# LSH attention into a soft mixture of experts: work on key tiles placed one by one, a 72-column transpose operand, and a new issue order

## The chip, the cores and the metric

The kernel runs on one core of one Trainium2 chip. The metric is the device time of one execution in microseconds (us); less is better. The engines are PE (TensorE; PEld is its weight load), DVE (VectorE), ACT (ScalarE), POOL (GpSimd) and SP (SyncE, which issues the DMAs here).

## What is computed

For each of B·H = 32 heads (S = 768 tokens, D = 64) queries and keys are hashed to 6 sign bits by a projection. A query attends only to keys with the same six bits:

```python
mask = q_bucket[:, :, :, None] == k_bucket[:, :, None, :]
scores = scale * np.matmul(q, k.transpose(0, 1, 3, 2))
scores = np.where(mask, scores, -1000000000.0)
attn = softmax(scores)            # with 1e-9 in the denominator
x = attn @ v                      # then (3072, 512)
logits = x @ phi                  # 8 experts x 4 slots
slot_input = softmax(logits, axis=0).T @ x
slot_out[e] = relu(slot_input[e] @ w1[e]) @ w2[e]
out = softmax(logits, axis=1) @ slot_out
```

## The kernel before

**Tiling.** The 768 keys of a head are six tiles of 128. Scores are held with keys on partitions and queries along the row, so that the exponentials go straight into the product with v. Heads are worked on in pairs (an even one and the odd one after it), since a transfer of queries and keys brings both. The 512-column PSUM buffers hold pieces of 512, 256 + 256 and 512 columns of two key tiles.

**Steps of a head.** `load` brings a pair's queries and keys. `bits` (line 328, four 32-column products in a 32-column shape of the array) and line 321 make the hash signs. `split_hi` (ACT, line 290) and `split_lo` (DVE, line 294) split the values into a rounded high part and a low rest in the tile w (w4); the `spread_*` DMAs (issued at line 298) lay these and the bits out in one of three operand tiles XY. `smax` (line 370) computes a first round of masked scores, whose maxima DVE reduces (lines 373 and 376) into mx. `shift` (lines 382, 383, 385, DVE) makes from mx a 128-row tile mz of 12 columns, six with the negative maximum and six with a large number where nothing matched. `shift_rows` turns mz by a transpose (line 404), ACT copies the turned rows (line 407), and a DMA puts them as one row into XY, so that the second product, `scores` (line 419), has the shift in it. ACT takes the exponential (line 423) into three tiles pt, each for two key tiles. `acc` keeps the running sum of the exponentials over key tiles on GpSimd (line 429 for the first two, line 435 for the others); `av` multiplies them with v (line 446, two 64-column halves of the array) and ACT copies the result (line 450).

**Steps of a pair.** `pair_sum` (line 458) sums over partitions, `pair_turn` (493), `pair_rec` (465), `pair_log` (473), `pair_add` (485, 487) and `pair_x` (508 on PE, 510 on DVE) divide by the sum and make x and its logits. After each eight heads the `batch_*` steps fold a batch into running slot inputs. Behind the last head come the experts (lines 829 to 953). Their weights are loaded by SP while the heads run, as buffers come free.

**The order.** Nothing is scheduled by a compiler. Every step is entered by `at` into a list with a number, its place in units of one key tile (six a head), the list is sorted, and each engine gets its instructions in that order and works through them in it. The table WHEN holds the numbers relative to a head's first slot (two lists where even and odd heads differ), FIRST replaces some of them for the first and the last heads. `acc` and `av` are entered three times a head, once for each two key tiles.

Of the kernel before, what the change touches and what calls it, by code (L numbers as in the profile page):

```python
# [44 lines left out]
WHEN = {'load': -23.228,
 'bits': -14.718,
 'split_hi': -14.15,
 'split_lo': [-13.173, -12.657],
 'spread': [[-13.185, -11.633, -9.493, -7.304], [-10.44, -10.41, -11.057, -10.018]],
 'load_v': [-3.955, -4.754],  # L50
 'smax': [[-7.721, -7.546, -7.104, -6.759, -6.183, -5.672, -5.543, -5.94, -4.42, -4.667, -3.989, -3.458],
          [-7.807, -7.787, -7.71, -7.157, -7.093, -4.763, -4.509, -5.317, -2.787, -3.873, -3.838, -5.786]],
 'scores': [[-0.379, -0.64, 0.722, 1.221, 1.676, 1.813, 4.783, 5.371, 5.128, 2.397, 4.882, 5.891],
            [0.479, 0.475, 0.687, 1.928, 1.817, 1.633, 2.087, 3.051, 4.451, 4.142, 4.29, 3.884]],
 'shift': [-2.803, -2.153],
 'shift_rows': [-2.18, -2.143],
 'acc': [[4.764, 7.001, 8.685], [3.578, 3.949, 8.203]],
 'av': [[3.488, 6.789, 7.032], [3.202, 4.62, 6.466]],
 'pair_sum': 15.98,
 'pair_turn': 17.963,  # L60
 'pair_rec': [18.062, 18.408, 18.445],
 'pair_log': 18.701,
 'pair_x': [22.593, 24.311],
 'pair_add': 19.165,
 'batch_both': 21.266,
 'batch_max': 21.916,
 'batch_exp': 22.194,
 'batch_turn': 23.394,
 'batch_scale': 23.246,
 'batch_slots': 24.562,  # L70
 'batch_weigh': 24.425,
 'batch_share': 28.126,
 'load_weights': 4.18}

FIRST = {('load', 4): 4.476,
 ('bits', 2): 1.288,
 ('split_hi', 2): 0.833,
 ('split_lo', 2, 0): 1.029,
 ('split_lo', 2, 1): 2.366,
 ('spread_y', 2): 1.587,  # L80
 ('spread_bits', 2): 1.668,
 ('spread_l', 2): 2.667,
 ('spread_x', 2): 3.34,
 ('smax', 1, 0, 0): -1.746,
 ('smax', 1, 0, 1): -1.169,
 ('smax', 1, 1, 0): 0.452,
 ('smax', 1, 1, 1): 0.57,
 ('smax', 1, 2, 0): 1.478,
 ('smax', 1, 2, 1): 1.593,
 ('smax', 1, 3, 0): 2.035,  # L90
 ('smax', 1, 3, 1): 2.061,
 ('smax', 1, 4, 0): 2.241,
 ('smax', 1, 4, 1): 2.696,
 ('smax', 1, 5, 0): 2.774,
 ('smax', 1, 5, 1): 3.433,
 ('one_sum', 30): 189.395,
 ('one_log', 30): 188.431,
 ('one_fold', 3): 189.992,
 ('one_turn', 30): 189.777,
 ('one_rec', 30): 190.438,  # L100
 ('one_add', 30): 190.708,
 ('one_x', 30): 191.23,
 ('one_put', 30): 192.78,
 ('acc', 31, 2): 192.109,
 ('av', 31, 2, 0): 191.864,
 ('av', 31, 2, 1): 192.733,
 ('first_y', 1): -20.551,
 ('first_y', 2): -3.524,
 ('spread_y', 1): -14.012,
 ('spread_l', 0): -12.047,  # L110
 ('spread_bits', 1): -7.869,
 ('bits_rest',): -7.878,
 ('bits_copy',): -13.916}


def constants():
# [31 lines left out]
def lsh_attention_soft_moe(  # L148
# [228 lines left out]

    def shift(h):
        s = st[h]
        mz = mp.tile([P, 2 * NT], F32, name="mz", bufs=2)  # L380
# [1 line left out]
        nc.vector.tensor_reduce(out=m, in_=s["mx"], axis=AX.X, op=ALU.max)
        nc.vector.tensor_scalar(out=mz[:, NT:2 * NT], in0=m, scalar1=NOMATCH, scalar2=BIG,  # L383
                                op0=ALU.is_lt, op1=ALU.mult)
        nc.vector.scalar_tensor_tensor(out=mz[:, 0:NT], in0=m, scalar=-1.0, in1=mz[:, NT:2 * NT],
                                       op0=ALU.mult, op1=ALU.subtract)
        s["mz"] = mz

    def shift_rows(h):
        s = st[h]  # L390
# [13 lines left out]
        nc.tensor.transpose(pt[0:2 * NT, 0:P], s["mz"], ident)  # L404

        mr = mp.tile([2 * NT, P], F32R, name="mr", bufs=1)
        nc.scalar.copy(mr, pt[0:2 * NT, 0:P])  # L407
        move(s["XY"][ROW:ROW + 1, 0].rearrange("o y (t p) -> o (y t) p", p=P), mr)
# [14 lines left out]
            nc.scalar.activation(s["P", i // 2][:, 512 * u:512 * u + 512], pt, AF.Exp, scale=D ** -0.5)  # L423

    def acc(h, j):
        s = st[h]
        pr = s["P", j]
        if j == 0:
            nc.gpsimd.tensor_tensor(out=s["acc"], in0=pr[:, 0:S], in1=pr[:, S:2 * S], op=ALU.add)  # L429
        else:  # L430
            for a in range(2):
                n = 2 * j + a
                eng = nc.vector if h == BH - 1 and n > 2 else nc.gpsimd
                if h < BH - 1 or n < NT - 1:
                    eng.tensor_tensor(out=s["acc"], in0=s["acc"], in1=pr[:, a * S:(a + 1) * S], op=ALU.add)  # L435

    def av(h, j, half=None):
        s = st[h]
        if j == 0:
            s["av"] = p_av.tile([P, 512], F32, name="av")  # L440
        pr = s["P", j]
        for i in (2 * j, 2 * j + 1):
            o = (i % 2) * S
            for c in range(2):
                if half in (None, i % 2):
                    nc.tensor.matmul(s["av"][64 * c:64 * c + 64, 0:HC], s["v"][:, i, :],  # L446
                                     pr[:, o + c * HC:o + (c + 1) * HC], start=(i == 0), stop=(i == NT - 1))
# [277 lines left out]
    for h in range(BH):  # L725
        s0, x = NT * h, h % 2
        if x == 0:
            if h > 0:
# [8 lines left out]
        for n in range(2 * NT):
# [1 line left out]
            at(s0 + WHEN["scores"][x][n], scores, h, n // 2, n % 2)  # L739
        at(s0 + WHEN["shift"][x], shift, h)  # L740
        at(s0 + WHEN["shift_rows"][x], shift_rows, h)
        for j in range(NT // 2):
            lone = h == BH - 1 and j == NT // 2 - 1
            at(s0 + (5.725 if lone else WHEN["acc"][x][j]), acc, h, j)
            if lone:
                for n in range(2):
                    at(s0 + 5.85 + n, av, h, j, n)
            else:
                at(s0 + (WHEN["av"][x][j] if h < BH - 1 else (3.513, 5.087)[j]), av, h, j)
# [257 lines left out]
```

## Time and profile before

| | us |
|---|---|
| time, median of 3 runs | 516.64 (516.59 to 516.72) |
| span of the profiled execution | 515.0, 1.64 less than that median |
| PE busy | 494.8 (96%) |
| DVE busy | 381.7 (74%) |
| GpSimd (POOL) busy | 327.6 (64%) |
| ACT busy | 241.2 (47%) |

The profiled execution is one run of its own, of which the profiler gives the span: from the first instruction to the end of the last, without what lies around it in a run's time. Busy times of an engine are those of its instructions; they overlap between engines, and matmuls are pipelined, so that on PE the distance from one start to the next says more than a duration. [...]

### The profile page before, as it was taken

Reading aid. Unit: us, or ns where it says so; the run is one execution under the profiler, and the core shown is the slowest. Engines: PE = TensorE matmul, PEld = TensorE weight load, DVE = VectorE, ACT = ScalarE, POOL = GpSimd, SP = SyncE. Lnnn points to the kernel's source line nnn. Section 1 sums busy time; section 2 is a strip of 40 time slices with the busy share of each in tenths; the row PEclk is TensorE's granted clock in tenths of the full one; section 3 lists DMA queues with packets and bytes.
Section 4 is the critical chain, followed back from the end, with each engine's and each line's share of the span. In section 5 each row is a group of like instructions: output and inputs, shape, how many; then the busy total and the mean of one; then the engine's idle time right before and its main releaser. Section 6 shows DMA issues by size and latency. Waiting matters only on the chain.

```text
span 515.0 us, 9100 instructions
## 1 busy us (share of the span) xinstructions
PE 494.8 (96%) x3164; PEld 289.1 (56%) x3164; DVE 381.7 (74%) x703; ACT 241.2 (47%) x463; POOL 327.6 (64%) x223
## 2 busy tenths in 40 slices
PE   6989999999999999999999999999999999999992
PEld 4555556565655555555656555555555655563562
DVE  5585877888888889797887887888877875464233
ACT  4145545454554455554564545454645545422242
POOL 9238776768676867677687867776678686512200
PEclk9789999999999999999999999999999999999997
DMA  5766766758675768586765675867455465869967
GB/s 127 203 137 151 201 161 194 175 163 192 198 161 160 185 186 196 177 191 180 180 191 140 171 197 143 229 146 222 101 145 132 93 169 197 327 264 389 409 270 277
DMA packets 39778, 99.60 MB, mean 193 GB/s; under 512 B 7458, under 2 KB 13732, under 8 KB 39732
## 3 DMA queue, kind: packets, MB, share of 16 engines
q1 hardware_dynamic: 39540, 98.94, 67.8%
q8 instruction: 25, 0.41, 0.3%
q14 instruction: 21, 0.17, 0.1%
q0 software_dynamic: 192, 0.08, 0.1%
HBM read 52.76 MB, written 6.29 MB: 115 GB/s over the span
## 4 chain that ended last, share of the span: by engine, by line
PE 78%; DVE 10%; DMA 5%; SPq 2%; ACT 2%; issue 1%; DVEq 0%; ACTq 0%
PE st L419 23%; PE av L446 21%; PE smx L370 14%; DVE mx L376 3%; PE qs L930 3%; PE qh L848 3%; DMA XY<-w 3%; DVE mx L373 2%; PE mi L458 2%; PE mi L473 2%; PE mi L328 2%; PE mi L508 2%; PE mi L404 1%; SPq L298 1%; DMA w<-w 1%
## 5 line engine op out<-in xcount | busy, mean ns | idle before, releaser
L435 POOL TENSOR_TENSOR acc<-acc,pt 128x768 f32<-128x768 f32 x125 | 238.5, 1908 | 68.5 <-ACT pt L423 54.7
L423 ACT ACTIVATE pt<-st 128x512 f32<-128x512 f32 x288 | 156.6, 596 | 60.5 <-PE st L419 49.3
L419 PE MATMUL st<-XY 128*128 128x256 f32 (+1 forms) x768 | 175.0, 342 | 0.8 <-ACT pt L423 0.5
L376 DVE TENSOR_REDUCE mx<-smx 128x1 f32<-128x512 f32 x192 | 129.4, 682 | 43.6 <-PE smx L370 43.1
L446 PE MATMUL av<-pt,v 128*64 128x384 f32 x768 | 143.1, 501 | 0.0
L419 PEld LDWEIGHTS st<-XY 128*128 128x128 f32 x768 | 123.2, 189 | 19.4 <-ACT pt L423 4.1
L370 PE MATMUL smx<-XY 96*128 96x512 f32 (+1 forms) x384 | 122.9, 374 | 5.2 <-DVE mx L376 3.9
L370 PEld LDWEIGHTS smx<-XY 96*128 96x128 f32 x384 | 65.3, 190 | 55.5 <-issue 16.4
L446 PEld LDWEIGHTS av<-pt,v 128*64 128x64 f32 x768 | 48.2, 137 | 65.7 <-issue 57.6
L429 POOL TENSOR_TENSOR acc<-pt 128x768 f32<-128x768 f32 x32 | 58.3, 1823 | 35.4 <-ACT pt L423 34.9
L373 DVE TENSOR_REDUCE mx<-smx 128x2 f32<-128x512 f32 x96 | 65.2, 679 | 8.5 <-PE smx L370 7.7
L450 ACT COPY avs<-av 128x384 f32<-128x384 f32 x32 | 15.3, 478 | 60.3 <-PE av L446 60.3
L465 DVE RECIPROCAL sm<-sm 128x128 f32<-128x128 f32 x45 | 38.4, 908 | 0.0
L294 DVE TENSOR_TENSOR w<-raw,w 128x768 fp32r<-128x768 f32 x30 | 36.3, 1210 | 1.9 <-ACT w L290 1.7
L407 ACT CAST mr<-mi 12x128 fp32r<-12x128 f32 x31 | 7.9, 254 | 62.7 <-PE mi L404 56.3
L290 ACT CAST w<-raw 128x768 fp32r<-128x768 f32 x32 | 25.1, 831 | 13.7 <-DMA v<-vt 8.2
L510 DVE TENSOR_TENSOR xq<-mi,r 128x256 f32<-128x256 f32 x45 | 17.4, 414 | 2.2 <-PE mi L508 1.2
L487 DVE TENSOR_TENSOR lacc<-lacc,sm 128x384 f32<-128x384 f32 x11 | 18.2, 1656 | 0.4
L321 DVE TENSOR_SCALAR bt<-mi,con 128x384 fp32r<-128x384 f32 x15 | 10.1, 677 | 10.8 <-PE mi L328 7.6
L383 DVE TENSOR_SCALAR mz<-m 128x6 f32<-128x6 f32 x32 | 15.0, 468 | 1.1
L328 PE MATMUL mi<-raw,pb 128*32 128x384 f32 x128 | 15.1, 517 | 0.5 <-DMA raw<-qk 0.5
L930 PE MATMUL qs<-w 128*32 128x256 f32 x232 | 15.2, 382 | 0.0
(173 smaller groups left out, 342.0 us busy)
## 6 DMA issues: line engine op xcount, KB each, us to landing
w<-w SPq DMA_DIRECT2D x61, 512.0 KB
XY<-w SPq DMA_DIRECT2D x63, 384.0 KB
raw<-qk SPq DMA_DIRECT2D x32, 384.0 KB
XY<-w SPq DMA_DIRECT2D x64, 192.0 KB
v<-vt SPq DMA_DIRECT2D x32, 192.0 KB
out<-w SPq DMA_DIRECT2D x12, 512.0 KB
xq<-w SPq DMA_DIRECT2D x3, 512.0 KB
XY<-bt SPq DMA_DIRECT2D x62, 19.5 KB
```

The source lines that it names most:

```text
L294: (nc.vector if h else nc.gpsimd).tensor_tensor(out=w[:, 2 * x + 1], in0=st[h]["raw"][:, x], in1=w[:, 2 * x], op=ALU.subtract)
L328: nc.tensor.matmul(pts_b[j // 2 if h == 0 else 0][32 * j:32 * j + 32, 0:HC], pb[:, 32 * (j // 2):32 * (j // 2) + 32], st[h]["raw"][:, j // ...
L370: nc.tensor.matmul(pt[:, o:o + b - a], s["Y"][0:96, 0, t * P:(t + 1) * P], s["Y"][0:96, 1, a:b], start=True, stop=True)
L373: nc.vector.tensor_reduce(out=mx[:, n - 1:n + 1], in_=pt.rearrange("p (a x) -> p a x", a=2), axis=AX.X, op=ALU.max)
L376: nc.vector.reduce_max(out=mx[:, n:n + 1], in_=pt, axis=AX.X)
L419: nc.tensor.matmul(pt[:, o:o + b - a], x[:, 1, i * P:(i + 1) * P], x[:, 0, a:b], start=first, stop=not first)
L423: nc.scalar.activation(s["P", i // 2][:, 512 * u:512 * u + 512], pt, AF.Exp, scale=D ** -0.5)
L429: nc.gpsimd.tensor_tensor(out=s["acc"], in0=pr[:, 0:S], in1=pr[:, S:2 * S], op=ALU.add)
L435: eng.tensor_tensor(out=s["acc"], in0=s["acc"], in1=pr[:, a * S:(a + 1) * S], op=ALU.add)
L446: nc.tensor.matmul(s["av"][64 * c:64 * c + 64, 0:HC], s["v"][:, i, :], pr[:, o + c * HC:o + (c + 1) * HC], start=(i == 0), stop=(i == NT - 1))
L465: nc.vector.reciprocal(out=rs[:, k * P:(k + 1) * P], in_=rs[:, k * P:(k + 1) * P])
L930: nc.tensor.matmul(po[32 * j:32 * j + 32], hTs[g][:, f, 32 * j:32 * j + 32], wt[1, x, 2 * g + f // 4, j][:, (f % 4) * HM:(f % 4 + 1) * HM] ...
```

## The change

It has three parts.

1. `acc` and `av` take one key tile at a time, so each of the six products with v and each of the five sums of a head has its own place.
2. mz becomes one tile of 128 × 72, set to zero once, used by all heads in place of two turning buffers of 128 × 12. The transpose takes all 72 columns and puts out 72 rows; the copy behind it still takes 12.
3. All numbers of WHEN and FIRST are new. The places of the last heads' steps move from FIRST and from the plan's own exceptions into a table LAST, counted from the end.

```diff
-WHEN = {'load': -23.228,
...
- 'split_lo': [-13.173, -12.657],
...
- 'acc': [[4.764, 7.001, 8.685], [3.578, 3.949, 8.203]],
- 'av': [[3.488, 6.789, 7.032], [3.202, 4.62, 6.466]],
...
+WHEN = {'load': -21.8018,
...
+ 'split_lo': [-12.086, -11.9126],
...
+ 'acc': [[3.6064, 6.5396, 7.1238, 7.1276, 7.3962], [2.2728, 3.8636, 4.3631, 5.3042, 6.9234]],
+ 'av': [[4.0843, 4.1824, 6.6951, 6.8065, 7.2516, 7.4705], [2.6288, 2.6313, 2.6452, 5.9656, 6.0723, 6.3287]],
...
+    mz_wide = mp.tile([P, 72], F32, name="mz")
+    nc.vector.memset(mz_wide, 0.0)
...
     def shift(h):
         s = st[h]
-        mz = mp.tile([P, 2 * NT], F32, name="mz", bufs=2)
+        mz = mz_wide
...
-        nc.tensor.transpose(pt[0:2 * NT, 0:P], s["mz"], ident)
+        nc.tensor.transpose(pt[0:72, 0:P], s["mz"], ident)
...
-    def acc(h, j):
-        s = st[h]
-        pr = s["P", j]
-        if j == 0:
+    def acc(h, n):
+        s = st[h]
+        pr = s["P", n // 2]
+        a = n % 2
+        if n == 1:
             nc.gpsimd.tensor_tensor(out=s["acc"], in0=pr[:, 0:S], in1=pr[:, S:2 * S], op=ALU.add)
-        else:
-            for a in range(2):
-                n = 2 * j + a
-                eng = nc.vector if h == BH - 1 and n > 2 else nc.gpsimd
-                if h < BH - 1 or n < NT - 1:
-                    eng.tensor_tensor(out=s["acc"], in0=s["acc"], in1=pr[:, a * S:(a + 1) * S], op=ALU.add)
-
-    def av(h, j, half=None):
+        elif h < BH - 1 or n < NT - 1:
+            eng = nc.vector if h == BH - 1 and n > 2 else nc.gpsimd
+            eng.tensor_tensor(out=s["acc"], in0=s["acc"], in1=pr[:, a * S:(a + 1) * S], op=ALU.add)
+
+    def av(h, i):
...
-        pr = s["P", j]
-        for i in (2 * j, 2 * j + 1):
-            o = (i % 2) * S
-            for c in range(2):
-                if half in (None, i % 2):
-                    nc.tensor.matmul(s["av"][64 * c:64 * c + 64, 0:HC], s["v"][:, i, :],
-                                     pr[:, o + c * HC:o + (c + 1) * HC], start=(i == 0), stop=(i == NT - 1))
+        pr = s["P", i // 2]
+        o = (i % 2) * S
+        for c in range(2):
+            nc.tensor.matmul(s["av"][64 * c:64 * c + 64, 0:HC], s["v"][:, i, :],
+                             pr[:, o + c * HC:o + (c + 1) * HC], start=(i == 0), stop=(i == NT - 1))
...
-        for j in range(NT // 2):
...
+        for n in range(NT):
+            if n:
+                at(s0 + WHEN["acc"][x][n - 1], acc, h, n)
+            at(s0 + WHEN["av"][x][n], av, h, n)
```

Line numbers in what follows are those of the kernel before; in the changed kernel line 294 is 303, 370 is 379, 373 and 376 are 382 and 385, 382, 383 and 385 are 391, 392 and 394, 404 is 413, 419 is 428, 446 is 451, 458 is 463, 508 and 510 are 513 and 515.

**How the order moves.** PE in the middle of the program, in the kernel before, from the bits of a pair on (mi is a shared PSUM buffer, avs the product with v, raw the loaded pair; `x4` is four instructions of the program):

```order
L419 MATMUL st<-XY_135 128x512 x2
L446 MATMUL av<-pt_81,v_88 64x384 x4
L328 MATMUL mi<-raw,pb 32x384 x4
L404 MATMUL mi<-ident,mz 12x128
L419 MATMUL st<-XY_135 128x512 x2
...
L508 MATMUL mi<-ident,avs 128x128 x4
L446 MATMUL av<-pt_82,v_88 64x384 x4
L370 MATMUL smx<-XY_134 128x512 x2
...
L508 MATMUL mi<-ident,avs 128x128 x2
L446 MATMUL av<-pt_83,v_88 64x384 x4
```

The same place of the changed kernel:

```order
L428 MATMUL st<-XY_137 128x512 x2
L451 MATMUL av<-pt_81,v_90 64x384 x4
L451 MATMUL av<-pt_82,v_90 64x384 x2
L337 MATMUL mi<-raw,pb 32x384 x4
L413 MATMUL mi<-ident,mz 72x128
...
L513 MATMUL mi<-ident,avs 128x128 x4
L379 MATMUL smx<-XY_136 128x512
L428 MATMUL st<-XY_135 128x256 x2
L379 MATMUL smx<-XY_136 128x512
L513 MATMUL mi<-ident,avs 128x128 x2
L451 MATMUL av<-pt_82,v_90 64x384 x2
L451 MATMUL av<-pt_83,v_90 64x384 x4
```

One product of the odd head's third key tile has moved ahead of the bits, and the other three tiles stand together behind the second group of transposes, where before they stood in two groups.

DVE at the same place in the kernel before, from the signs of the bits to the shift of the odd head:

```order
L321 TENSOR_SCALAR bt<-mi,con 128x384
...
L510 TENSOR_TENSOR xq<-mi,r 128x2x2x64 x2
L294 TENSOR_TENSOR w_2445<-raw,w_2445 128x768
L376 TENSOR_REDUCE mx<-smx 128x1 x2
L294 TENSOR_TENSOR w_2445<-raw,w_2445 128x768
L376 TENSOR_REDUCE mx<-smx 128x1
L510 TENSOR_TENSOR xq<-mi,r 128x2x2x64
...
L382 TENSOR_REDUCE m<-mx 128x6
L383 TENSOR_SCALAR mz<-m 128x6
L385 SCALAR_TENSOR_TENSOR mz<-m,mz 128x6
```

And of the changed kernel:

```order
L330 TENSOR_SCALAR bt<-mi,con 128x384
...
L515 TENSOR_TENSOR xq<-mi,r 128x2x2x64 x2
L385 TENSOR_REDUCE mx<-smx 128x1 x2
L515 TENSOR_TENSOR xq<-mi,r 128x2x2x64
L303 TENSOR_TENSOR w_2439<-raw,w_2439 128x768 x2
L385 TENSOR_REDUCE mx<-smx 128x1
...
L391 TENSOR_REDUCE m<-mx 128x6
L392 TENSOR_SCALAR mz<-m 128x6
L394 SCALAR_TENSOR_TENSOR mz<-m,mz 128x6
```

The two subtractions of `split_lo` stood apart, ahead of the last product with xq; they now follow each other behind it.

More of the change, by code (lines that the diff above doesn't have):

```diff
@@ L42 @@
 C_ALL = C_FD + P
-WHEN = {'load': -23.228,
- 'bits': -14.718,
- 'split_hi': -14.15,
- 'split_lo': [-13.173, -12.657],
[L49 to L56, printed above, removed]
- 'acc': [[4.764, 7.001, 8.685], [3.578, 3.949, 8.203]],
- 'av': [[3.488, 6.789, 7.032], [3.202, 4.62, 6.466]],
[L59 to L113, printed above, removed]
+WHEN = {'load': -21.8018,
+ 'bits': -14.6691,
+ 'split_hi': -14.2853,
+ 'split_lo': [-12.086, -11.9126],
+ 'spread': [[-12.4667, -11.7321, -3.899, -5.7625], [-11.417, -10.357, -9.3692, -10.6895]],
+ 'load_v': [-0.8721, -3.4246],
+ 'smax': [[-7.725, -7.6362, -7.528, -7.4981, -6.9757, -6.1053, -6.061, -6.7072, -7.2423, -4.5232, -4.1316, -3.8939], [-8.328, -7.6424, -7.5359, -7.1845, -6.5214, -4.6177, -3.7809, -4.7595, -2.8548, -3.3893, -3.3878, -6.2227]],
+ 'scores': [[0.9515, -0.4543, 1.633, 1.9165, 2.3728, 2.4911, 3.0605, 4.6359, 4.4841, 3.8281, 4.4315, 4.8794], [1.4707, -0.6271, -0.3487, -0.3744, 2.3577, -0.2831, 2.1001, 1.735, 4.7414, 4.0169, 4.3968, 3.5778]],
+ 'shift': [-2.7834, -2.656],
+ 'shift_rows': [-2.4257, -1.8003],
+ 'acc': [[3.6064, 6.5396, 7.1238, 7.1276, 7.3962], [2.2728, 3.8636, 4.3631, 5.3042, 6.9234]],
+ 'av': [[4.0843, 4.1824, 6.6951, 6.8065, 7.2516, 7.4705], [2.6288, 2.6313, 2.6452, 5.9656, 6.0723, 6.3287]],
+ 'pair_sum': 16.2251,
+ 'pair_turn': 17.1902,
+ 'pair_rec': [17.4431, 18.8499, 18.6658],
+ 'pair_log': 18.0362,
+ 'pair_x': [22.8563, 23.8597],
+ 'pair_add': 19.4762,
+ 'batch_both': 19.7926,
+ 'batch_max': 20.7183,
+ 'batch_exp': 20.8646,
+ 'batch_turn': 23.4977,
+ 'batch_scale': 24.9516,
+ 'batch_slots': 27.8808,
+ 'batch_weigh': 27.8111,
+ 'batch_share': 31.3776,
+ 'load_weights': 4.7959}
@@ new lines @@
+FIRST = {('load', 4): 6.1873,
+ ('bits', 2): -2.2549,
+ ('split_hi', 2): 1.1394,
+ ('split_lo', 2, 0): 1.6786,
+ ('split_lo', 2, 1): 4.0998,
+ ('spread_y', 2): 2.2047,
+ ('spread_bits', 2): -0.4924,
+ ('spread_l', 2): 3.553,
+ ('spread_x', 2): 6.2847,
+ ('smax', 1, 0, 0): -0.9212,
+ ('smax', 1, 0, 1): -0.2391,
+ ('smax', 1, 1, 0): 0.552,
+ ('smax', 1, 1, 1): 0.5993,
+ ('smax', 1, 2, 0): 0.9451,
+ ('smax', 1, 2, 1): 1.0559,
+ ('smax', 1, 3, 0): 1.6372,
+ ('smax', 1, 3, 1): 1.163,
+ ('smax', 1, 4, 0): 2.3368,
+ ('smax', 1, 4, 1): 1.9867,
+ ('smax', 1, 5, 0): 2.963,
+ ('smax', 1, 5, 1): 3.1611,
+ ('first_y', 1): -10.3221,
+ ('first_y', 2): -4.0536,
+ ('spread_y', 1): -12.6224,
+ ('spread_l', 0): -10.5924,
+ ('spread_bits', 1): -5.5442,
+ ('bits_rest',): -6.6899,
+ ('bits_copy',): -13.3252}
@@ new lines @@
+LAST = {('one_sum', -2): -3.9123,
+ ('one_log', -2): -3.9152,
+ ('one_fold', -1): -1.3861,
+ ('one_turn', -2): -3.4247,
+ ('one_rec', -2): -2.8241,
+ ('one_add', -2): -0.6243,
+ ('one_x', -2): -0.497,
+ ('one_put', -2): 0.8086,
+ ('acc', -1, 1): -2.9493,
+ ('acc', -1, 2): -1.9094,
+ ('acc', -1, 3): -1.7394,
+ ('acc', -1, 4): -0.3743,
+ ('acc', -1, 5): -11.8896,
+ ('av', -1, 0): -3.31,
+ ('av', -1, 1): -3.1119,
+ ('av', -1, 2): -3.0149,
+ ('av', -1, 3): -0.5227,
+ ('av', -1, 4): 1.6538,
+ ('av', -1, 5): 1.6814}
@@ L423, in scores @@
             nc.scalar.activation(s["P", i // 2][:, 512 * u:512 * u + 512], pt, AF.Exp, scale=D ** -0.5)
-    def acc(h, j):
+    def acc(h, n):
         s = st[h]
-        pr = s["P", j]
-        if j == 0:
+        pr = s["P", n // 2]
+        a = n % 2
+        if n == 1:
             nc.gpsimd.tensor_tensor(out=s["acc"], in0=pr[:, 0:S], in1=pr[:, S:2 * S], op=ALU.add)
-        else:
-            for a in range(2):
-                n = 2 * j + a
-                eng = nc.vector if h == BH - 1 and n > 2 else nc.gpsimd
-                if h < BH - 1 or n < NT - 1:
-                    eng.tensor_tensor(out=s["acc"], in0=s["acc"], in1=pr[:, a * S:(a + 1) * S], op=ALU.add)
-    def av(h, j, half=None):
+        elif h < BH - 1 or n < NT - 1:
+            eng = nc.vector if h == BH - 1 and n > 2 else nc.gpsimd
+            eng.tensor_tensor(out=s["acc"], in0=s["acc"], in1=pr[:, a * S:(a + 1) * S], op=ALU.add)
+    def av(h, i):
         s = st[h]
-        if j == 0:
+        if i == 0:
             s["av"] = p_av.tile([P, 512], F32, name="av")
-        pr = s["P", j]
-        for i in (2 * j, 2 * j + 1):
-            o = (i % 2) * S
-            for c in range(2):
-                if half in (None, i % 2):
-                    nc.tensor.matmul(s["av"][64 * c:64 * c + 64, 0:HC], s["v"][:, i, :],
-                                     pr[:, o + c * HC:o + (c + 1) * HC], start=(i == 0), stop=(i == NT - 1))
-        if j == NT // 2 - 1 and half != 0:
+        pr = s["P", i // 2]
[3 more added lines that the diff above has]
+                             pr[:, o + c * HC:o + (c + 1) * HC], start=(i == 0), stop=(i == NT - 1))
+        if i == NT - 1:
             s["avs"] = dp.tile([P, HC], F32, name="avs", bufs=3)
@@ L710, in lsh_attention_soft_moe @@
     plan = []
+    last = NT * BH
     def at(when, f, *args):
         key = (f.__name__, *(a for a in args if isinstance(a, int)))
-        plan.append((FIRST.get(key, when), len(plan), (f, *args)))
+        if key in FIRST:
+            when = FIRST[key]
+        elif len(key) > 1:
+            back = (key[0], key[1] - (B if f is one_fold else BH)) + key[2:]
+            when = last + LAST[back] if back in LAST else when
+        plan.append((when, len(plan), (f, *args)))
     first_y(0)
@@ L741, in lsh_attention_soft_moe @@
         at(s0 + WHEN["shift_rows"][x], shift_rows, h)
-        for j in range(NT // 2):
[L743 to L749, printed above, removed]
+        for n in range(NT):
+            if n:
+                at(s0 + WHEN["acc"][x][n - 1], acc, h, n)
+            at(s0 + WHEN["av"][x][n], av, h, n)
         if x and h < BH - 1:
@@ L762, in lsh_attention_soft_moe @@
                 at(p0 + WHEN[f.__name__], f, h // H)
-    last, h = NT * BH, BH - 1
+    h = BH - 1
     at(last - 3.2, one_sum, h - 1, p_mi)
```

## The prediction

> **What bounds the kernel now.** I read the page's busy times first, then the table by stage, then the engines' own lists of instructions over one period of the loop.
>
> ```profile
> span 515.0 us, 9100 instructions
> PE 494.8 (96%) x3164; PEld 289.1 (56%) x3164; DVE 381.7 (74%) x703; ACT 241.2 (47%) x463; POOL 327.6 (64%) x223
> PE 78%; DVE 10%; DMA 5%; SPq 2%; ACT 2%; issue 1%; DVEq 0%; ACTq 0%
> 40.00:440.00 400.00, 397.54 (x2360) 232.77 (x2356) 325.75 (x563) 203.93 (x390) 293.07 (x165) 1.00 0.66 173
> ```
>
> The first three lines are from the page, the last is the stage table (PE, PEld, DVE, ACT and POOL busy, then the clock). Between 40 and 440 us PE is busy for 397.54 of 400 us at a granted clock of 1.00. So time can come out of the middle only if PE issues less or changes shape less often; and whatever makes PE wait there goes into the span at full price. The profiled span is 515.0 us, 1.6 below the median of the runs, 516.64; I sum changes against the span and add them to the median.
>
> One period handles a pair of heads. I mark in it C, the turn of the even head's shift (line 404, just behind the hash bits), and A, the turn of the odd head's shift (line 404 again, ahead of the sum of the previous pair). PE around one such stretch:
>
> ```profile
> 285.89 0.28 PE L404 MATMUL mi<-ident,mz 128*12 128x128 f32 x1
> 287.06 0.41 PE L419 MATMUL st<-XY 128*128 128x256 f32 x2
> 287.30 0.28 PE L370 MATMUL smx<-XY 96*128 96x256 f32 x1
> 287.42 0.63 PE L419 MATMUL st<-XY 128*128 128x512 f32 x2
> 287.89 0.60 PE L508 MATMUL mi<-ident,avs 128*128 128x128 f32 x4
> 288.42 1.51 PE L446 MATMUL av<-pt,v 128*64 128x384 f32 x8
> 289.86 0.74 PE L370 MATMUL smx<-XY 96*128 96x512 f32 x2
> 290.44 0.88 PE L419 MATMUL st<-XY 128*128 128x256 f32 x4
> 296.03 1.51 PE L446 MATMUL av<-pt,v 128*64 128x384 f32 x8
> 297.60 0.28 PE L404 MATMUL mi<-ident,mz 128*12 128x128 f32 x1
> ```
>
> From C (285.89) to A (297.60) is 11.71 us. What a visit to the 64-column shape of line 446 costs can be read off. Two 512-column steps between full shapes take 287.89 - 287.42 = 0.47; the two behind the visit take 290.44 - 289.86 = 0.58, 0.11 more. Ahead of it four transposes take 288.42 - 287.89 = 0.53; their own step is (0.60 - 0.28)/3 = 0.107, from a group of four and a lone one, so 0.43, and the entry costs 0.10. And inside, sixteen issues of line 446 in a row take less than two visits of eight:
>
> ```profile
> 38.89 2.80 PE L446 MATMUL av<-pt,v 128*64 128x384 f32 x16
> 41.62 0.61 PE L370 MATMUL smx<-XY 96*128 96x256 f32 x2
> ```
>
> That is 41.62 - 38.89 = 2.73 against 2 x 1.44 (288.42 to 289.86), 0.15 less. A visit costs 0.11 + 0.10 + 0.15 = 0.36 us beyond its work. The Trainium skill says, in TensorEngine Tiling (Array Packing), under Performance Considerations, that a change of tiling mode drains the array; the 0.36 here is its price in this kernel.
>
> Ahead of A, the last visit takes 297.60 - 296.03 = 1.57, not 1.44: PE waits 0.13 there, for this:
>
> ```profile
> PEld mi L404 <- DVE mz L385: 20.0, 28, 1.2
> 286.03 0.68 DVE L321 TENSOR_SCALAR bt<-mi,con 128x384 fp32r<-128x384 f32 x1 [0.49 <-PE mi L328]
> 287.14 0.69 DVE L376 TENSOR_REDUCE mx<-smx 128x1 f32<-128x512 f32 x1 [0.43 <-PE smx L370]
> 287.75 0.68 DVE L373 TENSOR_REDUCE mx<-smx 128x2 f32<-128x512 f32 x1
> 288.53 0.75 DVE L510 TENSOR_TENSOR xq<-mi,r 128x256 f32<-128x256 f32 x2
> 289.20 0.95 DVE L294 TENSOR_TENSOR w<-raw,w 128x768 fp32r<-128x768 f32 x1
> 290.40 1.29 DVE L376 TENSOR_REDUCE mx<-smx 128x1 f32<-128x512 f32 x2 [0.26 <-PE smx L370]
> 291.61 1.81 DVE L294 TENSOR_TENSOR w<-raw,w 128x768 fp32r<-128x768 f32 x1
> 293.94 0.41 DVE L510 TENSOR_TENSOR xq<-mi,r 128x256 f32<-128x256 f32 x1
> 294.87 1.48 DVE L373 TENSOR_REDUCE mx<-smx 128x2 f32<-128x512 f32 x2
> 296.98 0.17 DVE L382 TENSOR_REDUCE m<-mx 128x6 f32<-128x12 f32 x1
> 297.38 0.17 DVE L385 SCALAR_TENSOR_TENSOR mz<-m,mz 128x6 f32<-128x6 f32 x1
> ```
>
> The first line is of the list of waits (most of its 20.0 us is the weight load's, hidden behind PE's own work); the others are DVE between C and A. DVE finishes the shift at 297.55 and the turn starts at 297.60. So A hangs on DVE. And one operation there has two durations: the low half's subtraction of line 294 took 0.95 and then 1.81. GpSimd tells why:
>
> ```profile
> 285.39 3.77 POOL L435 TENSOR_TENSOR acc<-acc,pt 128x768 f32<-128x768 f32 x2
> 290.78 4.33 POOL L435 TENSOR_TENSOR acc<-acc,pt 128x768 f32<-128x768 f32 x2 [1.63 <-ACT pt L423]
> 295.25 1.82 POOL L429 TENSOR_TENSOR acc<-pt 128x768 f32<-128x768 f32 x1
> 154.72 1.49 DVE L294 TENSOR_TENSOR w<-raw,w 128x768 fp32r<-128x768 f32 x1
> L294 DVE TENSOR_TENSOR w<-raw,w x30: 946/1054/2047, 26.5 to 400.2; 128x768 fp32r<-128x768 f32 x30
> 284.37 0.97 DVE L383 TENSOR_SCALAR mz<-m 128x6 f32<-128x6 f32 x1
> ```
>
> With GpSimd idle (289.16 to 290.78) the subtraction took 0.95. The one at 291.61 met the add that began at 290.78; the two adds then took 4.33 together where 3.77 is usual, because the second waited in its turn. Thirty subtractions run from 0.946 to 2.047. The tiny line 383 took 0.97 while an add was running, and line 382, just ahead of A, 0.17. So DVE and GpSimd keep each other out, instruction by instruction. The Trainium skill has this rule in SBUF — State Buffer, under Who interferes with whom: a DVE operation with two SBUF inputs, or in a two-port mode, and a GpSimd operation that reads SBUF hold a shared port pair for a whole instruction, whoever issues first. The trace agrees (0.95 against 1.81), and the rule speaks against this change.
>
> **The change part by part.** *Products with v.* By the issue order the visits to the 64-column shape fall from five a pair to four; over the whole program changes of shape go from 250 to 228. By visits that is 0.36 a pair; by changes, 22 x 0.18 = 4.0 us, 0.26 a pair. I take 0.29, nearer the count, since that has every place in it: 15 pairs give -4.3 us. In the end stretch I put one visit, -0.4.
>
> *The 72-column operand.* Its transpose keeps its neighbours: behind products with v or bits, ahead of the 32-column sums or the scores. It loads 72 columns in place of 12; line 404's own turn is 0.28 like any other 128-column step. No row has the 72 columns in front of these neighbours: between -0.1 (an entry saved) and +0.05 a turn, I take 0. The memset is one small instruction at the start. One shared buffer in place of two asks line 392 to wait for the turn before, over ten us earlier.
>
> *The running sum.* The same adds, but no longer behind two key tiles at once. In before the add of key tile 4 begins at 290.78, C + 4.89, right behind the third exponential:
>
> ```profile
> 287.61 1.57 ACT L290 CAST w<-raw 128x768 fp32r<-128x768 f32 x2 [1.15 <-DMA XY<-w]
> 289.08 1.56 ACT L423 ACTIVATE pt<-st 128x512 f32<-128x512 f32 x3
> ```
>
> Now one exponential stands ahead of the two casts of line 290 and the add needs only the second; two exponentials earlier, 2 x 0.52, gives C + 3.85. The add of tile 3 ended at 289.16, C + 3.27, so I put the add of tile 4 at C + 4.0 to 5.83 (1.83 each), the add of tile 5 right behind.
>
> *DVE and PE from C to A.* PE: 11.71, less 0.13 waited, less one visit 0.36, less two key tiles of v moved ahead of C, (2.73 - 1.44)/2 = 0.64, and two more 256-column score steps, 2 x 0.12 (287.06 to 287.30): 10.8 us. DVE: both subtractions now stand together behind all three products with xq. Up to them: 0.14 (285.89 to 286.03), 0.68, then 0.69 + 0.68 + 0.68 for reductions, 0.75, 1.29, 0.41: C + 5.32. That is inside the add of tile 4. Free of GpSimd: 2 x 0.95 to 7.22, reductions 0.68 + 1.48 + 0.68 to 10.06, shift 0.57 (296.98 to 297.55) and 0.05 to the turn: 10.68. So the slack against PE is 0.12 us; more lock wait than that stops PE, with the weight load of A in the queue and the sums of the previous pair, then smax, behind it.
>
> The wait: the first subtraction starts at 5.83, not 5.32, 0.51 lost. If DVE keeps the lock for the second, both end at 7.73; the add of tile 5 runs 7.73 to 9.56, the next head's first add 9.56 to 11.39. Line 392 of the shift is asked for at 7.73 + 2.84 + 0.20 = 10.77, inside that add, and loses 0.62, or nothing if the add is a little late. A comes at 11.19 or 11.81: PE waits 0.39 or 1.01, and the errors of my three chained starts are as large as the difference; I take the middle, 0.70. Per pair: -0.29 - 0.13 + 0.70 = +0.28; times 15, +4.2; with the end, +3.8.
>
> *Cover that gets thinner.* The row of shifts sent by DMA after C had 290.44 - 285.89 = 4.55 us until its head's first scores; in the new order the steps between add up to 2.9. Its cast and its issue are through by about C + 1.4:
>
> ```profile
> 286.48 0.81 SPq L298 DMA_DIRECT2D XY<-mr  x1
> ```
>
> So 1.5 us remain for the landing; no row gives that, I cost it at nothing and let the range bear some. The other transfers of SP's queue keep their number and size. In the first 40 us reductions and subtractions trade places: PE's 1.5 us wait for line 376 at 28.7 may go, or a like one come; I take 0.
>
> **The rivals.** *No lock wait in the window* (0.35). If the adds fall beside the subtractions, or DVE gets ahead of them, DVE stays within the 0.12 of slack: -0.29 - 0.13 = -0.42 a pair, -6.3, with the end -6.7: 509.9 us. For it: half of before's subtractions took under 1.054, and the shift ahead of A took 0.17. Against: the adds of tiles 4 and 5 cover C + 4 to 7.7 without a gap, and 5.32 is in the middle.
>
> *GpSimd takes the lock between the two subtractions* (0.14), the slower side's sharp form. At 154.72 a subtraction got in between two queued adds; by the same turn-taking a queued add gets in between two subtractions. First to 6.78, add of tile 5 to 8.61, second to 9.56, shift asked at 12.6; A at 13.0, or 13.6 if one more add stands there: PE waits 2.2 to 2.8, +1.8 to +2.4 a pair, +27 to +36: near 547 us. It decides where the add of tile 5 is ready before the first subtraction ends, at C + 6.8.
>
> *Nothing comes of it* (0.07). The visits saved come back as costs of the 72 columns or as a wait for the shift's row at 2.9 us: within 1 us or so of 516.6.
>
> **How the numbers follow.** The forecast (0.44) is 516.64 + 3.8 = 520.4 us; its own range, with shift lost or not, is 15 x (-0.03) - 0.4 = -0.9 to 15 x 0.59 - 0.4 = +8.5, 515.8 to 525. About 0.2% (1 us) is what a measurement of this kernel can tell. Of the forecast's 0.44 I put 0.05 faster, 0.08 the same, 0.31 slower; of the last rival 0.02 faster and 0.05 the same. Faster 0.35 + 0.05 + 0.02 = 0.42, same 0.13, slower 0.31 + 0.14 = 0.45. The range 508.5 to 530 holds all but the sharp form and some tails.
>
> **What would show it.** Right: in the new profile the two subtractions take 2.4 us or more together, line 392 ahead of A near 0.8 in some pairs, PE idle ahead of line 413 by 0.4 to 1.0 a pair, and 64-column visits at four a pair with a period near 26.3 us. Subtractions at 0.95 each and a period of 25.6 would prove the first rival; an add between the subtractions and 28 us the second. I am wrong in the terms themselves if PE waits elsewhere, above all behind the shift's row or at the scores.

## The result

| | before | changed |
|---|---|---|
| time, median of 4 runs | 516.62 us (516.53 to 516.72) | 550.97 us (546.62 to 553.09) |
| ratio | | 1.0655, 95% interval 1.061 to 1.0701 |
| span of the profiled execution | 515.0 us | 548.4 us |

The changed kernel is 34.35 us slower, 6.6%. One run of experiment 6, at 532.29 us, was in a slower state and is left out of that experiment's figures. The prediction had 520.4 us with a range to 530; the time that came out is that of its second rival (near 547 us), which it had given 0.14.

### The profile page after: what moved, and what is told of

It reads as the page before. It is cut to its first block, busy times and chain, and to the rows that moved or that the text cites. A ratio compares the mean times of both kernels' runs of the same rounds, so it can differ in the third digit from the quotient of the medians.

```text
span 548.4 us, 8987 instructions
## 1 busy us (share of the span) xinstructions
PE 502.6 (92%) x3164; PEld 296.3 (54%) x3164; DVE 406.2 (74%) x704; ACT 246.6 (45%) x463; POOL 333.3 (61%) x223
## 4 chain that ended last, share of the span: by engine, by line
PE 62%; DVE 29%; DMA 3%; issue 1%; ACT 1%; POOL 1%; SPq 0%; DVEq 0%; POOLq 0%; ACTq 0%
PE st L428 17%; PE av L451 16%; DVE w L303 11%; PE smx L379 9%; DVE mx L385 7%; DVE mx L382 4%; DVE mz L392 3%; PE qs L937 3%; PE qh L855 3%; PE mi L463 2%; PE mi L478 2%; DVE xq L515 2%; PE mi L337 2%; DMA w<-w 2%; PE mi L413 2%
## 5 line engine op out<-in xcount | busy, mean ns | idle before, releaser
L432 ACT ACTIVATE pt<-st 128x512 f32<-128x512 f32 x288 | 162.3, 596 | 65.5 <-PE st L428 57.9
L428 PE MATMUL st<-XY 128*128 128x256 f32 (+1 forms) x768 | 186.2, 347 | 0.4 <-DMA XY<-mr 0.4
L379 PE MATMUL smx<-XY 96*128 96x512 f32 (+1 forms) x384 | 132.7, 374 | 20.6 <-DVE mx L385 18.4
L428 PEld LDWEIGHTS st<-XY 128*128 128x128 f32 x768 | 125.8, 191 | 33.7 <-issue 20.0
L379 PEld LDWEIGHTS smx<-XY 96*128 96x128 f32 x384 | 69.4, 191 | 50.2 <-DVE mx L385 28.6
L439 POOL TENSOR_TENSOR acc<-pt 128x768 f32<-128x768 f32 x32 | 64.2, 2008 | 26.8 <-ACT pt L432 26.4
L303 DVE TENSOR_TENSOR w<-raw,w 128x768 fp32r<-128x768 f32 x30 | 60.1, 2040 | 0.0
L392 DVE TENSOR_SCALAR mz<-m 128x6 f32<-128x6 f32 x32 | 26.0, 814 | 1.1
L330 DVE TENSOR_SCALAR bt<-mi,con 128x384 fp32r<-128x384 f32 x15 | 10.1, 677 | 18.4 <-PE mi L337 16.2
L413 PEld LDWEIGHTS mi<-ident,mz 128*72 128x72 f32 x31 | 3.6, 115 | 31.7 <-DVE mz L394 22.4
L413 PE MATMUL mi<-ident,mz 128*72 128x128 f32 x31 | 9.8, 315 | 9.6 <-DVE mz L394 9.5
```

What stands on the lines that cost most here:

```text
L303: (nc.vector if h else nc.gpsimd).tensor_tensor(out=w[:, 2 * x + 1], in0=st[h]["raw"][:, x], in1=w[:, 2 * x], op=ALU.subtract)
L379: nc.tensor.matmul(pt[:, o:o + b - a], s["Y"][0:96, 0, t * P:(t + 1) * P], s["Y"][0:96, 1, a:b], start=True, stop=True)
L428: nc.tensor.matmul(pt[:, o:o + b - a], x[:, 1, i * P:(i + 1) * P], x[:, 0, a:b], start=first, stop=not first)
```

## The profile after

The page of the changed kernel: the span, the engines, the chain that ended last, and three groups of section 5.

```profile
span 548.4 us, 8987 instructions
PE 502.6 (92%) x3164; PEld 296.3 (54%) x3164; DVE 406.2 (74%) x704; ACT 246.6 (45%) x463; POOL 333.3 (61%) x223
PE 62%; DVE 29%; DMA 3%; issue 1%; ACT 1%; POOL 1%; SPq 0%; DVEq 0%; POOLq 0%; ACTq 0%
L303 DVE TENSOR_TENSOR w<-raw,w 128x768 fp32r<-128x768 f32 x30 | 60.1, 2040 | 0.0
L392 DVE TENSOR_SCALAR mz<-m 128x6 f32<-128x6 f32 x32 | 26.0, 814 | 1.1
L413 PE MATMUL mi<-ident,mz 128*72 128x128 f32 x31 | 9.8, 315 | 9.6 <-DVE mz L394 9.5
```

PE has the same 3164 instructions as before and is busy for 92% of the span instead of 96%; DVE's share of the chain rises from 10% to 29%. The subtraction (303, before 294) takes 2040 ns on average instead of 1210, the small step of the shift (392, before 383) 814 instead of 468, and PE sits idle for 9.6 us ahead of the turn (413). That is not the longest of PE's waits: the first of the two lines below, from its list of waits (us in total, times, longest), is smax (line 379) waiting for a reduction (385) that has yet to read one of its two PSUM buffers; the page of before has 3.9 us of it.

```profile
PE smx L379 <- DVE mx L385: 18.4, 16, 1.8
PE mi L413 <- DVE mz L394: 9.5, 12, 1.3
```

In the lists of instructions that follow `x2` joins neighbours of one kind, and each of the program's 384 products with v shows as two instructions (768 of line 451).

One pair on DVE and on GpSimd, from the first product with xq after C to the shift ahead of A (the same steps as in the stretch that the prediction showed, in a pair whose C is at 337.67 and A at 351.80):

```profile
340.74 0.75 DVE L515 TENSOR_TENSOR xq<-mi,r 128x256 f32<-128x256 f32 x2
341.41 1.28 DVE L385 TENSOR_REDUCE mx<-smx 128x1 f32<-128x512 f32 x2
342.60 0.41 DVE L515 TENSOR_TENSOR xq<-mi,r 128x256 f32<-128x256 f32 x1
342.93 4.54 DVE L303 TENSOR_TENSOR w<-raw,w 128x768 fp32r<-128x768 f32 x2
347.40 0.68 DVE L385 TENSOR_REDUCE mx<-smx 128x1 f32<-128x512 f32 x1
350.19 1.35 DVE L392 TENSOR_SCALAR mz<-m 128x6 f32<-128x6 f32 x1
351.57 0.17 DVE L394 SCALAR_TENSOR_TENSOR mz<-m,mz 128x6 f32<-128x6 f32 x1
```

```profile
342.34 4.32 POOL L442 TENSOR_TENSOR acc<-acc,pt 128x768 f32<-128x768 f32 x2 [2.75 <-ACT pt L432]
346.62 2.53 POOL L439 TENSOR_TENSOR acc<-pt 128x768 f32<-128x768 f32 x1
349.70 1.81 POOL L442 TENSOR_TENSOR acc<-acc,pt 128x768 f32<-128x768 f32 x1 [0.55 <-ACT pt L432]
```

Two subtractions that need 0.95 each take 4.54 us together. Read it against GpSimd: the first is issued at 342.93, inside the add that began at 342.34; it can run only when that ends, near 344.2. The second is issued right behind the first, but the next add has been waiting and goes first; the two adds together take 4.32 instead of 3.75. Then the third add waits in its turn (346.62, 2.53 instead of 1.82). At the shift one more add stands in the way: 1.35 us for an operation of 0.17. DVE's shift is done at 351.74 and PE's turn starts at 351.80. But PE had stopped before that: the reduction at 347.40 had to wait behind the second subtraction, and smax behind the reduction, from 346.31 to 348.13.

PE at the three turns, and at that smax:

```profile
337.67 0.30 PE L413 MATMUL mi<-ident,mz 128*72 128x128 f32 x1
348.13 0.50 PE L379 MATMUL smx<-XY 96*128 96x256 f32 x2 [1.82 <-DVE mx L385]
351.80 0.43 PE L413 MATMUL mi<-ident,mz 128*72 128x128 f32 x1
367.28 0.30 PE L413 MATMUL mi<-ident,mz 128*72 128x128 f32 x1
```

C to A is 14.13 us here (11.71 in the pair shown of before), A to C 15.48 (14.81 in most pairs of this run; here a stretch at half clock falls into it, see below), the period 29.61. Over the whole middle, from the C at 48.41 to the C at 425.81, are 13 periods of 29.03 us; in before 13 periods from 46.60 to 394.44 give 26.76. The difference is 2.27 us a pair, 29.6 us in these 13. Of the 33.4 us by which the two spans differ, 1.8 lie ahead of them and 2.0 behind, so the loss lies in the pairs.

A smaller second part shows in the clock. The stage table of the changed kernel at two places:

```profile
117.60:121.00 3.40, 3.40 (x13) 1.49 (x11) 2.89 (x5) 0.60 (x1) 2.27 (x2) 0.53 0.75 279
350.00:353.40 3.40, 3.35 (x15) 0.58 (x11) 1.67 (x3) 0.26 (x1) 1.51 (x1) 0.51 0.43 162
```

The column behind the busy times is the granted clock: 0.5 for about 3.4 us. There are four such stretches between 40 and 510 us of the changed kernel (at 60, 118, 234 and 350 us) and none in before, whose clock in 40 to 440 us was 1.00. Work in one loses at most half of its 3.4 us, so the four are 6.8 us at most.

## The experiments

Each ratio is to the kernel before, run on the same chip in the same set. C, A and the period are as above; "clean" pairs are those without a batch's steps. Lines of the runs' own copies differ by a few. Where an edit is shown in part, `...` marks it.

### 1. The two subtractions apart

```diff
- 'split_lo': [-12.086, -11.9126],
+ 'split_lo': [-13.1, -12.18],
+ ('split_lo', 0, 0): -12.086,          # first pair as it was
+ ('split_lo', 0, 1): -11.9126,
```

> The changed kernel with only the places of the two subtractions changed, to stand as before among DVE's work: the first behind the first two products with xq, the second two reductions later. Lock theory: the first one starts near C + 3.7 us, ahead of the add of key tile 4 (C + 4.7), and takes 0.95; the second meets that one add and waits up to 0.6; so of the 2 to 3 us that a pair lost, 0.5 to 1 stays, and the time is 515 to 527. Rival (the loss lies in the rest of the new order: finer products with v, the shift's row, the scores): the time stays above 540.

Measured: 517.47 us, ratio to before 1.0025 (1.0011 to 1.0038). Two numbers undo 33 of the 34 us. The subtractions in this run (least, median and longest ns), then PE's turns in a clean pair:

```profile
L305 DVE TENSOR_TENSOR w<-raw,w x30: 945/950/2259, 28.2 to 400.0; 128x768 fp32r<-128x768 f32 x30
```

```profile
313.95 0.30 PE L415 MATMUL mi<-ident,mz 128*72 128x128 f32 x1
325.04 0.30 PE L415 MATMUL mi<-ident,mz 128*72 128x128 f32 x1
339.85 0.30 PE L415 MATMUL mi<-ident,mz 128*72 128x128 f32 x1
```

The median subtraction is back at 950 ns. C to A is 11.09, A to C 14.81; in the cleanest pairs C to A is 10.95 and the period 25.77, against 26.13 for the usual clean pair of before. So the new order is 0.36 us a pair shorter once DVE keeps up, as the prediction's first rival had it (-0.42). The sum is not below before all the same: three pairs lose 0.7 us each behind A (experiment 5), two others 0.8 and 1.7 ahead of it, and the first period is 1.4 us longer than in before (26.87 against 25.50).

### 2. The kernel before, with its subtractions side by side

```diff
- 'split_lo': [-13.173, -12.657],
+ 'split_lo': [-11.65, -11.64],
+ ('split_lo', 0, 0): -13.173,
+ ('split_lo', 0, 1): -12.657,
```

> The kernel before with the two subtractions side by side behind the third product with xq, as in the changed kernel; all else as before. Lock theory: the first meets the add of key tile 4, the add of key tile 5 gets in between, the second takes 2.6 us as in the changed kernel, and each pair grows by 2 to 2.8 us: 545 to 560. Rival (the rest of the new order makes the loss, the pairing of the subtractions little): 517 to 525.

Measured: 531.40 us, ratio 1.0289 (1.0269 to 1.031). Between the two theories: the pairing alone costs 15 us in the old order, but not 30. The second subtraction took 2.6 us in three pairs only (whose first one starts at 52.81, 82.51 and 330.75), and 0.95 elsewhere. In those three the first subtraction met the add of key tile 4, and that of tile 5 was next. In eight others the first subtraction came later than I expected, during the add of tile 5 itself; the next head's first add was not ready when it ended, and nothing was queued to get in between. In the last three, and in the first pair, whose places were kept, no add stood in the way. The rest of the loss came from the first subtraction (up to 2.56) and shows on PE at smax, which waited 16.2 us for a reduction that stands behind both. So the pairing needs another add queued behind the one that the first subtraction meets to cost its full price, and in the changed kernel there is one.

### 3. The changed kernel without one add

```diff
-        elif h < BH - 1 or n < NT - 1:
+        elif n < NT - 1:
```

> The changed kernel without the add of key tile 5 on GpSimd: that tile is left out of the running sum, so the softmax's denominators lack it. DVE's order, both subtractions side by side, is as in the changed kernel. Lock theory: nothing is queued on GpSimd that could get in between the subtractions, so the second takes 0.95 right behind the first; what stays is the wait of the first for the add of key tile 4 and perhaps one at the shift; the period falls from 29.2 to 25.7 to 26.6 and the time to 512 to 526. Rival (two subtractions in a row are late for another reason, such as their place behind the third product with xq): above 540.

The kernel leaves out the add of key tile 5 for every head, so its denominators lack that tile.

Measured: 532.01 us, ratio 1.0322 (1.0297 to 1.0348). The loss is 16 us over before in place of 34: 18 us went with that add. A pair of this run on DVE and GpSimd, C at 351.88:

```profile
357.15 2.27 DVE L303 TENSOR_TENSOR w<-raw,w 128x768 fp32r<-128x768 f32 x2
362.26 0.17 DVE L392 TENSOR_SCALAR mz<-m 128x6 f32<-128x6 f32 x1
362.46 1.65 DVE L394 SCALAR_TENSOR_TENSOR mz<-m,mz 128x6 f32<-128x6 f32 x1
```

```profile
355.93 1.81 POOL L442 TENSOR_TENSOR acc<-acc,pt 128x768 f32<-128x768 f32 x1 [2.12 <-ACT pt L432]
360.37 1.83 POOL L439 TENSOR_TENSOR acc<-pt 128x768 f32<-128x768 f32 x1 [2.64 <-ACT pt L432]
362.28 1.81 POOL L442 TENSOR_TENSOR acc<-acc,pt 128x768 f32<-128x768 f32 x1
```

The second subtraction now follows at once in every pair and takes 0.94 to 0.95 (2.27 for both in the pair shown), as expected. The time is above the range given, because of the shift: an add began at 362.28 while line 392 ran, and line 394, which also reads two operands from SBUF, waited it out for 1.65 us. I had counted a wait at 392 only and taken half of it. A clean pair has C to A of 12.2 to 13.1 here.

### 4. The operand of the turn

In the changed kernel, in experiment 1 and, the other way round, alone in the kernel before:

```diff
...
-        mz = mz_wide
+        mz = mp.tile([P, 2 * NT], F32, name="mz", bufs=2)
...
-        nc.tensor.transpose(pt[0:72, 0:P], s["mz"], ident)
+        nc.tensor.transpose(pt[0:2 * NT, 0:P], s["mz"], ident)
```

> The changed kernel with the turn's operand as before: two buffers of 128 x 12, 12 columns transposed. Lock theory (GpSimd's adds get in between the two subtractions of DVE and hold up the shift): nothing of it touches the operand, so the time stays within 3 us of 551. Operand theory (the 72 columns or the one shared buffer cost PE or DVE something at each of the 31 turns): the time falls, by 0.3 us a turn or 9 us and more if it is the main cause.

> The run with the two subtractions apart, and the turn's operand as before, two buffers of 128 x 12. The turn's PE step then changes the array's shape again in place of loading 72 columns. If the 72 columns gain something at the turn (an entry of 0.1 us saved), this is 1 to 3 us slower than the 72-column version beside it; if they cost the 115 ns weight load in place of 85, up to 1.5 us faster; the 5 us by which the changed kernel with 12 columns was under the changed kernel, on another chip, would have to show here as 5 us if the operand alone made it.

> The kernel before with the 72-column operand alone (one shared tile, set to zero once). Forecast of the prediction: between -0.1 and +0.05 us a turn, 31 turns, so 513 to 518.5 with 516 to 517 the likeliest. If the shared buffer made DVE wait for the turn before, or the turn cost more, it would be above 518.5.

> The changed kernel once more, unedited, for a comparison on the chip of these runs. With 12 columns it ran 545.75 on the chip of the first runs. If the operand makes 1.2 to 1.6 us here too, this is 546 to 549; if the 5 us between 545.75 and 550.97 were all the operand's, 550 to 552.

Measured: the changed kernel with 12 columns 545.75 us, ratio 1.0564 (1.0541 to 1.0586), and unedited once more 551.39, 1.0683 (1.0663 to 1.0703); experiment 1 with 12 columns 515.88, ratio 0.9998 (0.9984 to 1.0012), against 517.47 (ratio 1.0025) with 72 in another set of runs; before with 72 columns 517.14, ratio 1.0023 (1.0013 to 1.0034). So 72 columns cost 1.2 us in before. The clean period agrees: 26.13 becomes 26.17 in before, 25.77 becomes 25.69 when experiment 1 goes back to 12, that is 0.02 to 0.04 us a turn over 31 turns. In the stalled kernel the excess over before is 29.8 us with 12 columns and 34.9 with 72: the difference, 5.1, is more than the turns can be, and less than the 9 us expected if the operand were the main cause. The second run of the unedited kernel came out in the range that its expectation gave to the operand alone (550 to 552). The profiled runs differ in the clock there: five stretches at half clock between 40 and 510 us in the unedited one, two with 12 columns. Three stretches at 1.7 us at most are up to 5.1 us, enough for the rest. That the operand makes fewer of them was not shown: the first four runs of the changed kernel alone spread over 6.5 us.

### 5. The batch's maximum behind the shift

Experiment 1 left A to C at 15.5 us in three pairs. DVE in one of them, the end of a batch's first half standing ahead of the shift:

```profile
149.34 0.55 DVE L619 TENSOR_REDUCE ml<-dl 64x1 f32<-64x384 f32 x1 [0.96 <-POOL dl L611]
149.99 0.15 DVE L393 TENSOR_REDUCE m<-mx 128x6 f32<-128x12 f32 x1
150.17 1.05 DVE L394 TENSOR_SCALAR mz<-m 128x6 f32<-128x6 f32 x1
```

On top of experiment 1's edit:

```diff
- 'batch_max': 20.7183,
- 'batch_exp': 20.8646,
+ 'batch_max': 21.25,
+ 'batch_exp': 21.27,
```

> The run with the two subtractions apart, and the batch's maximum and exponential placed behind the even head's shift in place of ahead of it. In the run before this one DVE sat 0.96 us ahead of the maximum, waiting for GpSimd, with the shift behind it, and PE waited 0.7 at that turn in three pairs of batches. If that order makes the 15.5 us stretches from A to C, they become 14.8 and the time falls by 2 to 3 us, to 0.3 to 0.5% under the kernel before; if the lock at the shift makes them, nothing changes.

Measured: 514.78 us, ratio 0.9972 (0.9949 to 0.9994). The three stretches became 14.80, 14.82 and 14.83. With both edits and 12 columns:

> All three edits together on the changed kernel: the subtractions apart, the batch's maximum behind the shift, the turn's operand of 12 columns in two buffers. If the gains of the single runs add up (1.2 to 1.6 us for 12 columns, 1 to 2.7 us for the batch's place), 513 to 514, 0.4 to 0.6% under the kernel before. If the 12 columns gained only because the phases shifted, 514.5 to 516.

Measured: 514.61 us, ratio 0.9968 (0.995 to 0.9985), no further gain that the interval shows. It has the lowest time here, level with the version ahead of it and 0.3% under before. A clean pair has PE busy for all of its period:

```profile
339.96:365.66 25.70, 25.70 (x160) 15.64 (x157) 21.70 (x39) 14.39 (x27) 18.08 (x11) 1.00 0.70 185
```

### 6. One visit more

On that version, one product of v moved to a place of its own:

```diff
-[2.6288, 2.6313, 2.6452, 5.9656, 6.0723, 6.3287]
+[2.6288, 2.6313, 4.43, 5.9656, 6.0723, 6.3287]
```

These are the odd head's six places of `av`; the third moves.

> The run with the three edits, and the odd head's product with v of key tile 2 moved by two slots, out of its group ahead of the bits to a place of its own among full-shape steps: one visit to the 64-column shape more per pair, five as in the kernel before. By the prediction's price a visit costs 0.36 us, so 15 pairs give 5 us more than the run beside it, 518 to 519. If visits do not matter (PE has slack there, or DVE sets the period), it is within 1 us of it.

Measured: 524.82 us (five runs), ratio 1.0157 (1.0131 to 1.0183), more than either theory. PE's turns in a clean pair, without the edit and with it:

```profile
339.96 0.27 PE L413 MATMUL mi<-ident,mz 128*12 128x128 f32 x1
350.86 0.27 PE L413 MATMUL mi<-ident,mz 128*12 128x128 f32 x1
365.66 0.27 PE L413 MATMUL mi<-ident,mz 128*12 128x128 f32 x1
```

```profile
208.39 0.28 PE L413 MATMUL mi<-ident,mz 128*12 128x128 f32 x1
220.31 0.27 PE L413 MATMUL mi<-ident,mz 128*12 128x128 f32 x1
234.46 0.28 PE L413 MATMUL mi<-ident,mz 128*12 128x128 f32 x1
```

A period of 25.70 becomes 26.07: 0.37 us for one visit, where the prediction read 0.36 off the trace. That is 5.5 of the 10.2 us. The rest shows above all in three pairs outside the batches whose C to A is 14.2 to 14.8: in the one at 314.9 the first subtraction took 2.31 and line 392 1.35, the lock again, because the adds stand differently to DVE.

### 7. Two more places for the subtractions

```diff
- 'split_lo': [-12.086, -11.9126],      # the changed kernel
+ 'split_lo': [-13.1, -7.79],
- 'load': -21.8018,
+ 'load': -19.7,
...
+ ('split_lo', 0, 0): -12.086,
+ ('split_lo', 0, 1): -11.9126,
+ ('load', 2): -9.8018,
```

> The changed kernel with the first subtraction behind the first two products with xq and the second one moved past the odd head's shift, into the stretch where DVE has idle time; the next pair's load moves behind it. Lock theory: DVE has one subtraction less to do between C and A, so the shift is on time, the period is 25.5 to 26 us, and the time 507 to 517. Rival (rest of the new order): above 540. If the second subtraction now meets an add behind A, it costs up to 1.8 us of DVE's time where DVE has some 3 to spare, and PE little.

Measured: 570.53 us, ratio 1.1057 (1.0995 to 1.112): slower still, outside both ranges, for a new reason. Its chain by line has two steps of the queue that were no bound in the changed kernel:

```profile
PE st L431 18%; DMA XY<-w 12%; PE smx L382 11%; PE av L454 9%; SPq L310 9%; DVE mz L397 4%; DVE mx L388 3%; PE qs L940 3%; PE qh L858 3%; DVE mx L385 2%; PE mi L466 2%; DMA XY<-bt 2%; PE mi L516 2%; PE mi L481 1%; DVE mz L395 1%
```

The operand transfers out of w are late (12% DMA, 9% SP's issue). The later subtraction or the later load behind it held up SP's queue; which of the two was not taken apart. So the time neither bears out the lock theory nor speaks against it; the second subtraction, now far from the first, takes 0.94 to 0.95 us in twelve of its 15 pairs.

```diff
- 'split_lo': [-13.1, -12.18],          # the version with both edits and 12 columns
+ 'split_lo': [-12.8, -12.79],
...
-        (nc.vector if h else nc.gpsimd).tensor_tensor(
+        nc.gpsimd.tensor_tensor(
...
```

> The run with the three edits, and the subtractions taken from DVE and put on GpSimd, between the adds of key tiles 3 and 4, where GpSimd sat idle for 2.7 us in the changed kernel. DVE then has nothing of 768 columns to wait with, but GpSimd's adds of tiles 4 and 5 begin 3 us later and the shift ahead of A stands among them. Lock theory: the period is 25.6 to 26.5 (the shift can still wait up to 1.8 for an add): 508 to 522. If DVE's load and not the lock set the period, it would be faster than the run beside it by DVE's 1.9 us a pair at most, and PE's own work stops it near 25.5: 508 to 511.

Measured: 526.49 us, ratio 1.018 (1.0159 to 1.02), above both ranges. DVE is busy for 292 us between 40 and 440 in place of 317, and the kernel is 12 us slower: DVE's load was not the bound. What is left on DVE, the shift, waits for the adds, which now run later; PE waits for line 394 at 14 turns:

```profile
PE mi L413 <- DVE mz L394: 16.6, 14, 3.0
```

## Why the prediction was wrong

**What held.** PE's visits to the 64-column shape: 0.36 us forecast, 0.37 measured in experiment 6. (The drain at a change of tiling mode, which the prediction names there, stands in TensorEngine Tiling (Array Packing) of the Trainium skill under Key Properties.) The shorter C to A of PE: 10.8 forecast, 10.90 to 10.95 in clean pairs of experiments 1 and 5. Its term for v says two key tiles moved ahead of C, but 0.64 is the price of one, and one moved. DVE's arrival at the subtractions: C + 5.32 forecast, 342.93 - 337.67 = 5.26 measured, inside the add of key tile 4 as forecast. That DVE has next to no slack against PE there: in the list of PE's waits in the changed kernel none for another engine or a transfer adds up to more than 1.0 us.

**The step that failed** is "If DVE keeps the lock for the second": the forecast let both subtractions run before the add of tile 5. In all 14 pairs from the one at 52.78 us on the second subtraction took 2.59 to 2.61 us, with an add in between: that of tile 5 in twelve of them, in two, where the first subtraction came just ahead of it, that of tile 4. The prediction had the evidence in hand, at 154.72: a subtraction that had waited got in between two queued adds. By the same turn-taking a queued add gets in between two subtractions. I gave that 0.14 where the trace gave no reason for the other order at all. Its condition, the add of tile 5 ready before C + 6.8, was met: GpSimd took it up at C + 6.56, 0.08 us behind the add of tile 4. Experiment 3 shows the other side: with that add left out the second subtraction takes 0.95 in every pair.

**Where PE stops.** The forecast had PE waiting at A, for the shift. It stops earlier and, in sum, for longer: 18.4 us in 16 waits at smax, for a reduction behind the subtractions, against 9.5 us in 12 waits at the turn. The forecast counted the reductions as time of DVE's on the way to the shift, not as something that PE needs on its own way to A. The cause is the same late second subtraction.

**Sizes.** The rival's "near 547 us" fits: the period grew by 2.27 net of the 0.3 to 0.4 saved. That it fits so well is in part luck, since its 2.2 to 2.8 us of PE waiting a pair are more than was measured: PE is busy for 374.1 of the 400 us between 40 and 440, so it stands for 1.9 us a period. Stretches at half clock, which it did not have, are up to 0.5 a period; the small rest was not taken apart. The add of tile 4 began at C + 4.67, not 4.0, which made the first wait longer (1.1 us in the pair shown, 0.51 forecast). The shift's wait was larger than I let it be, since not only line 392 but also line 394 waits; experiment 3 shows 1.65 there.

**Operand and clock.** The 72 columns cost 0.02 to 0.04 us a turn, within the bounds given (-0.1 to +0.05), where I took 0. Stretches at half clock I had not counted; they are up to 6.8 of the 34 us, though where PE waits anyway they cost less. What brings them on was not shown: experiment 3 and the last run of experiment 7 have none between 41 and 440 us, though PE stands for 16.9 and 13.7 of the 400 us from 40 on. The page TensorE: Matmul & The Clock Gate of the Trainium skill says, in Part 1, that the array's clock drops to half after an idle window of about 3.4 us; the stretches here are 3.4 us long, but the longest wait in PE's list, 1.8 us (2.0 for its weight load), is shorter than such a window.

**The last rival** did not come: at the scores PE's list has 0.4 us in all of waiting for the shift's row.

## What to carry to other kernels

When two engines exclude each other instruction by instruction, an operation's price depends on what is queued on the other engine when it is issued: place two such operations of one engine apart, each where the other engine is idle, and not back to back while the other has work queued. An order that shortens the bounding engine's own work also shortens the time the others have, so count the slack of the engine that feeds each turn before crediting the gain. Where the profile shows who wins a contest once, use the same rule in the other direction instead of hoping for the better order.

## What the runs showed of the hardware

- DVE and GpSimd take turns, instruction by instruction, when both have work queued: two subtractions of 0.95 us and two adds of 1.82 us interleaved as add, subtraction, add, subtraction in twelve of 14 pairs of the changed kernel.
- An operation of 128 x 6 elements waits as long as a large one: line 392 took 0.17 or up to 1.77 us, line 394 0.17 or 1.65.
- The granted clock fell to half for 3.4 us at a time in some of the runs where PE waited: between 41 and 440 us none in before, in experiments 1, 3, 5 and 6 and in the last run of 7; one in experiment 2; two to five in the changed kernel and its 12-column form.
